# Where a block's score products stand: a RetNet and ELU-MLP kernel whose TensorE queue is full

## The chip, the cores and the metric

The kernel runs on one core of a Trainium2 chip. The metric is the time of one launch on the device, in microseconds (us); a version's time is the median over its runs. Everything is computed in 32-bit floating point.

## The reference

Two steps follow one another. The first is the recurrent form of retention, for 4 sequences of 768 tokens with 8 heads of 64:

```
for t in range(S):
    state = gamma * state + k[t] (outer product) v[t]      # per sequence and head, 64 x 64
    y[t]  = scale * q[t] @ state
```

with `gamma = 1 - 2 ** (-5 - h)` for head `h` and `scale = 1 / sqrt(64)`. The heads of a token are then put side by side, which gives a matrix `x` of 3072 tokens by 512. The second step is a two-layer perceptron with an ELU between its layers:

```
h = x @ w_in                                  # 512 -> 2048
g = where(h > 0, h, exp(min(h, 0)) - 1)
out = g @ w_out                               # 2048 -> 512
```

## The kernel before

**Blocks.** The 3072 tokens are cut into six blocks of 512 (`tb` 0 to 5; the text counts them from the first block, so the third block is `tb` 2). Each block is four chunks of 128 tokens, and a chunk is loaded as one 1024 KB transfer that holds q, k and v.

**Retention of a block** is done in pieces of 64 tokens and comes in five steps, which the function `retention_step(tb, step)` lists:

- step 0, scores: `scores(tb, pp)` for the two pairs of chunks, `pp` 0 and 1. Each makes 32 products of 64x64 on TensorE (L312) into two PSUM tiles `sc`, and two VectorE multiplications by the causal mask (L323) write the masked scores over the chunk's transposed k.
- step 1, states: 64x64 products k by v (L352) into PSUM tiles `kv`, and a chain of VectorE additions (L364) that sums the states of the pieces one after another.
- steps 2, 3 and 4, outputs: `outputs_step` multiplies scores by v (L408) and states by q (L423) into PSUM tiles `y`; small VectorE copies (`seen`, L392) stand in the first two steps, and in the last one four VectorE multiplications (L398) write the block's `x`.

The powers of gamma are put on v beforehand: `scale_v(m)` multiplies the v of chunk `m` by a table (L286), on VectorE for the third block and on GpSimd for later ones. The states of a block need its scaled v; the scores don't.

**The two GEMMs of a block** use Strassen's seven products, numbered 1 to 7, in one level or in two. In the second block the first GEMM is one level: `first(n)` for four slices `n` of w_in, each seven products of eight 128x256 matmul records (L758) in the order 1, 2, 6, 7, 5, 3, 4. The last two products of a slice are issued after the first two of the next slice. After each product ScalarE copies PSUM away (L704), VectorE adds (`h<-pd,m` and `h<-pb,m`, L709), ScalarE makes the exponential (L491, L492) and VectorE finishes the ELU (L495).

The second GEMM, `second_twice(tb, ...)`, has two levels: seven outer products in the order of `ORDER2`, 1, 2, 6, 7, 5, 3, 4, and in each of them seven inner ones of eight 128x128 records (L973). In what follows an outer product is called j1, j2, j6 and so on, and its inner ones k1, k2, k6, k7, k5, k3, k4; the last two again come after the first two of the next outer product. VectorE makes the sums of the inputs (`ts`, L847) and adds the results up (`res`, L985); between some outer products it also renews an input in place (L787). Each inner product takes a 256 KB piece of w_out from a ring of eleven buffers (`wq`), which SyncE fills.

**The order of the work** on each engine is the order in which the program is written: there is no scheduler. The third block's retention therefore stands where the code of the second block calls `retention_step(2, ...)`: at five visits in the second block's second GEMM, listed in `VISITS`. Later blocks have steps 0 and 1 inside their first GEMM (L931) and three visits in the second.

The PSUM tiles `sc`, `kv` and `y` rotate through a pool of four, `ps_r`. The GEMMs use four others: two named `pa`, one `pb` and one `pd`. A product that starts in `pd` has to wait until VectorE has read what was in it.

Of the kernel before, what the change touches and what calls it, by code (L numbers as in the profile page):

```python
# [18 lines left out]
def kernel(  # L19
# [45 lines left out]
    CPB = TB // C  # L65
# [33 lines left out]
    def load(m, cuts=(0, 2048), behind=None):  # L99

        if m >= NCHUNK:
            return
        t = ldpool.tile([P, 2048], FP32, name="chunk", tag="chunk")
        raw[m] = (
            t[:, 0:1024].rearrange("p (a h c) -> p a h c", a=2, c=C),
            t[:, 1024:2048].rearrange("p (a h d) -> p a h d", a=2, d=D),
        )
        hold(t, behind)
        for lo, hi in itertools.pairwise(cuts):
            nc.sync.dma_start(t[:, lo:hi], qkv[m, :, lo:hi])  # L110
# [169 lines left out]
    def scale_v(m, by_vector=False):  # L280
        if m >= NCHUNK:
            return
        i = chunks[m][1]
        v = raw[m][1][:, 0]
        eng = nc.vector if by_vector or m < 2 else nc.gpsimd
        eng.tensor_tensor(  # L286
            out=v, in0=v, in1=vf[:, i].unsqueeze(2).to_broadcast([C, H, D]), op=ALU.mult
        )
# [18 lines left out]
    def score_products(sc, tb, pp, x):  # L307
        qk = raw[tb * CPB + 2 * pp + x][0]
        for p in range(HP):
            for sub in range(2):  # L310
                for a in range(2):
                    nc.tensor.matmul(  # L312
                        sc[a][rows(sub), x, p, :], lhsT=qk[rows(a), 1, p, rows(sub)],
                        rhs=qk[rows(a), 0, p, rows(sub)], start=True, stop=True, skip_group_check=True,
                    )

    def scores(tb, pp):

        sc = [ps_r.tile([P, 2, HP, D], FP32, name="sc", tag="r") for _ in range(2)]
        for x in range(2):  # L320
            score_products(sc, tb, pp, x)
        for a in range(2):
            nc.vector.tensor_tensor(  # L323
                out=raw[tb * CPB + 2 * pp + a][0][:, 1].rearrange("p h c -> p (h c)").rearrange("p (n t) -> p n t", t=D),
                in0=sc[a].rearrange("p x h t -> p (x h) t"),
                in1=cmask.unsqueeze(1).to_broadcast([P, 2 * HP, D]), op=ALU.mult,
            )
# [38 lines left out]
    def states(tb, pp):  # L366

        kvs = [ps_r.tile([P, 2, HP, D], FP32, name="kv", tag="r") for _ in range(2)]
        for x in range(2):
            state_products(kvs, tb, pp, x, range(2))  # L370
        for x in range(2):
            for sub in range(2):
                state_sum(kvs, tb, pp, x, sub)
# [80 lines left out]
    def outputs_step(tb, step):  # L454

        if step == 0:
            held["y"] = [outputs(tb, pp) for pp in range(2)]
        if step < 2:
            next(held["y"][step])
            next(held["y"][step])  # L460
        else:
            for g in held["y"]:
                next(g, None)
# [18 lines left out]
    def flush():  # L482
        while later:
            later.pop(0)()
# [170 lines left out]
    def send_small():  # L655
        while to_send:
            nc.sync.dma_start(*to_send.pop(0))
# [41 lines left out]
    def bank(x):  # L699
        return ps_f.tile([P, 2, TH], FP32, name="p" + x, tag=x, bufs=2 if x == "a" else 1)  # L700
# [491 lines left out]
    def run(steps):  # L1192
        for _ in steps:
            pass
# [8 lines left out]
    def some(steps, count):  # L1203
        for _ in itertools.islice(steps, count):
            pass
# [78 lines left out]
    def retention_step(tb, step):  # L1284
        if tb >= NTB:
            return
        if step == 0:
            scores(tb, 0)
            scores(tb, 1)
        elif step == 1:  # L1290
            states(tb, 0)
            states(tb, 1)
        elif step < 5:
            outputs_step(tb, step - 2)
# [9 lines left out]
    for n in range(NQ):  # L1304
        if n < 3:
            load(2 * CPB + n)
        if n == 2:
            load(2 * CPB + 3)
        cur = first(n)
        for at in range(3):  # L1310
            next(cur)

        if n in (1, 2):
            some(smalls[n + 1], 1)
        elif n == 3:
            scale_v(2 * CPB, True)
        for _ in tail:
            pass
        for at, s in enumerate(cur):
            next(sides[n], None)  # L1320
            next(sides[n], None)
            if at == 1 and n in (0, 2):
                some(smalls[2 if n == 0 else 3], 2)
            elif at == 1 and n == 3:
                for m in range(1, CPB):
                    scale_v(2 * CPB + m, True)
            if s == "gap":
                break
        for _ in sides[n]:
            pass  # L1330
        tail = cur
        if n in (1, 2):
            run(smalls[n + 1])
        send_small()

    early.close()
    ring = ctx.enter_context(tc.tile_pool(name="ring", bufs=RING))
# [10 lines left out]
    for _ in tail:  # L1348
        pass
    flush()  # L1350
    step, VISITS = 0, [(0, "end"), (2, "middle"), (3, "first"), (4, "end"), (5, "end")]
    for s in sec:
        if s == "first":
            step += 1
        at = (step, s if s in ("first", "middle") else "end")
        if at in VISITS:
            retention_step(2, VISITS.index(at))
        if s == ORDER2[-1]:
            break
    tail = sec  # L1360
# [2 lines left out]
    for tb in range(2, NTB):  # L1363
        more = tb + 1 < NTB
        qa, qd, u2, end = {}, {}, {}, None

        def rest(n, j):
            if j == 1:
                qa[n] = ps_r.tile([P, 2, TH], FP32, name="qa", tag="r") if n == 0 else bank("a")
            if j == 7:  # L1370
                qd[n] = ps_r.tile([P, 2, TH], FP32, name="qd", tag="r") if n == 3 else bank("bd"[n % 2])
            first_rest(n, j, qa[n] if j in (1, 6, 5) else qd[n])

        def bring(n):
            if more:
                load((tb + 1) * CPB + n)
                scale_v((tb + 1) * CPB + n)

        def pop(count=1):
            for _ in range(count):  # L1380
                if later:
                    later.pop(0)()

        bring(0)
        rest(0, 1)
        for _ in tail:
            pass
        tail, parts = iter(()), combine_x_parts()
        for at, j in enumerate(TWICE):
            cur = first_twice(tb, j)  # L1390

            next(cur)
            next(tail, None)
            next(parts, None)
            next(cur)
            for _ in tail:
                pass
            next(parts, None)
            if at == 1:

                first_end(0, "C11", qa[0])()
                bring(1)
            next(cur)
            tail = cur
        next(tail)
        bring(2)

        sec = second_twice(tb, combine_x_twice if more else lambda: None)
        for n in range(NQ):

            rest(n, 6)
            u2[n] = kept(qa[n])
            if n == 0:
                for _ in tail:
                    pass
            if end:
                end()
            pop()
            rest(n, 7)
            m7 = kept(qd[n])  # L1420
            pop(2)
            if n == 2 and more:
                retention_step(tb + 1, 1)
            if n == 3:
                next(sec)
            rest(n, 5)
            end = first_end(n, "C12", qa[n])
            other = first_end(n, "C22", qa[n], m7)
            if n < 3:
                end()  # L1430
                other()
                rest(n + 1, 1)
                first_end(n + 1, "C11", qa[n + 1])()
                rest(n, 4)
                end = first_end(n, "C21", qd[n], u2[n])
                pop()
                if n == 0:
                    bring(3)
                elif n == 1 and more:
                    retention_step(tb + 1, 0)  # L1440
        for _ in range(2):
            next(sec)
        end()
        other()
        rest(3, 4)
        end = first_end(3, "C21", qd[3], u2[3])
        next(sec)
        end()
        flush()
        step = 0  # L1450
        for s in sec:

            if s == "first":
                step += 1
            elif s != "middle" and step in (1, 4, 5):
                retention_step(tb + 1, {1: 2, 4: 3, 5: 4}[step])
            if s == ORDER2[-1]:
                break
        tail = sec
# [51 lines left out]
```

## Time and profile before

| | us |
|---|---|
| median of 3 runs (lowest, highest) | 632.94 (632.79, 635.29) |
| the profiled execution | 633.48 |
| its span, first to last instruction | 631.6 |
| TensorE busy in the span | 623.8 |
| VectorE busy | 482.1 |
| ScalarE busy | 255.3 |
| GpSimd busy | 22.1 |

A time in the timeline is counted from the start of the span. A row of the timeline has the start, the duration, the engine, the line, the operation, the tiles written and read, the shape and the number of records that it merges; in brackets stands the idle time of the engine before it, and what ended it. Matmuls overlap, and their modelled ends lie a little past the start of the next one, so TensorE's own pace is read from the distance between starts. DVE is VectorE, ACT ScalarE, POOL GpSimd, PE TensorE, PEld its weight loads, and SP the queue of SyncE that issues the DMAs. Most products of a 32-bit matmul leave two records, so a product of four matmuls shows as eight.

### The profile page before, as it was taken

Reading aid. Unit: us, or ns where it says so; the run is one execution under the profiler, and the core shown is the slowest. Engines: PE = TensorE matmul, PEld = TensorE weight load, DVE = VectorE, ACT = ScalarE, POOL = GpSimd, SP = SyncE. Lnnn points to the kernel's source line nnn. Section 1 sums busy time; section 2 is a strip of 40 time slices with the busy share of each in tenths; the row PEclk is TensorE's granted clock in tenths of the full one; section 3 lists DMA queues with packets and bytes.
Section 4 is the critical chain, followed back from the end, with each engine's and each line's share of the span. In section 5 each row is a group of like instructions: output and inputs, shape, how many; then the busy total and the mean of one; then the engine's idle time right before and its main releaser. Section 6 shows DMA issues by size and latency. Waiting matters only on the chain.

```text
span 631.6 us, 16140 instructions
## 1 busy us (share of the span) xinstructions
PE 623.8 (99%) x6678; PEld 560.5 (89%) x6678; DVE 482.1 (76%) x882; ACT 255.3 (40%) x476; POOL 22.1 (4%) x30
## 2 busy tenths in 40 slices
PE   8999999999999999999999999999999999999997
PEld 6864578888899999888999989999989999988997
DVE  6688789989799665799585589777489877558975
ACT  6798646025541114553112646112465211366311
POOL 1021000000000000200000100000110000000000
PEclk9999999999999999999999999999999999999999
DMA  8698669699288788306888702889810698700794
GB/s 329 260 416 295 186 202 268 196 272 319 113 266 257 234 258 315 141 2 199 257 258 296 278 2 71 268 280 289 317 64 16 220 310 252 207 17 4 239 309 151
DMA packets 75897, 136.32 MB, mean 216 GB/s; under 512 B 6320, under 2 KB 31792, under 8 KB 70832
## 3 DMA queue, kind: packets, MB, share of 16 engines
q1 hardware_dynamic: 75824, 135.29, 64.9%
q8 instruction: 53, 0.87, 0.5%
q14 instruction: 20, 0.16, 0.1%
HBM read 114.03 MB, written 21.23 MB: 214 GB/s over the span
## 4 chain that ended last, share of the span: by engine, by line
PE 98%; DVE 0%; issue 0%; ACT 0%
PE pa L973 20%; PE pa L931 10%; PE pd L973 10%; PE pb L973 5%; PE pa L885 5%; PE pb L931 4%; PE pa L758 4%; PE pa L535 3%; PE qa L931 3%; PE x L625 3%; PE pd L885 2%; PE qd L931 2%; PE pd L931 2%; PE pd L758 2%; PE pa L625 2%; PE kv L352 2%
## 5 line engine op out<-in xcount | busy, mean ns | idle before, releaser
L981 ACT COPY ms<-pa 128x128 f32<-128x128 f32 x104 | 27.6, 265 | 148.2 <-PE pa L973 148.2
L973 PE MATMUL pa<-ts,wq 128*128 128x128 f32 x560 | 74.2, 275 | 0.0
L973 PE MATMUL pd<-ts,wq 128*128 128x128 f32 x552 | 73.5, 276 | 0.0
L973 PEld LDWEIGHTS pa<-ts,wq 128*128 128x128 f32 x560 | 68.5, 192 | 0.4
L973 PEld LDWEIGHTS pd<-ts,wq 128*128 128x128 f32 x552 | 67.1, 192 | 0.6 <-DVE res L985 0.2
L973 PE MATMUL pa<-gC,wq 128*128 128x128 f32 x480 | 64.6, 278 | 0.0
L492 ACT ACTIVATE r<-r 128x512 f32<-128x512 f32 x96 | 60.5, 631 | 3.1
L973 PEld LDWEIGHTS pa<-gC,wq 128*128 128x128 f32 x480 | 59.0, 192 | 1.3
L491 ACT ACTIVATE r<-gC 128x512 f32<-128x512 f32 x64 | 39.9, 624 | 31.9 <-DVE gC L939 31.9
L985 DVE TENSOR_TENSOR res<-pd,ms 128x128 f32<-128x128 f32 x68 | 19.5, 287 | 39.6 <-PE pd L973 38.4
L495 DVE SCALAR_TENSOR_TENSOR gC<-r,gC 128x512 f32<-128x512 f32 x64 | 42.6, 697 | 0.7 <-ACT r L492 0.7
L847 DVE TENSOR_TENSOR ts<-gC,ts 128x512 f32<-128x512 f32 x60 | 41.3, 688 | 1.0
L847 DVE TENSOR_TENSOR ts<-gC 128x512 f32<-128x512 f32 x60 | 41.0, 683 | 0.0
L286 POOL TENSOR_TENSOR chunk<-chunk,vf 128x512 f32<-128x512 f32 x16 | 19.4, 1212 | 429.6 <-DMA chunk<-in_qkv_dram 429.6
L973 PE MATMUL pb<-gC,wq 128*128 128x128 f32 x240 | 31.7, 275 | 0.0
L1006 ACT COPY res<-pa 128x128 f32<-128x128 f32 x34 | 9.0, 265 | 55.1 <-PE pa L973 55.1
L973 PEld LDWEIGHTS pb<-gC,wq 128*128 128x128 f32 x240 | 29.2, 192 | 0.0
L704 ACT COPY m<-pa 128x512 f32<-128x512 f32 x24 | 14.0, 582 | 33.0 <-PE pa L758 18.7
L939 DVE TENSOR_TENSOR gC<-qa,gC 128x512 f32<-128x512 f32 x8 | 5.5, 692 | 25.0 <-PE qa L931 18.3
L931 PE MATMUL pa<-xt,w_s 128*128 128x256 f32 x96 | 23.0, 382 | 0.0
L931 PE MATMUL pa<-xt,w_b 128*128 128x256 f32 x96 | 23.0, 382 | 0.0
L931 PE MATMUL pa<-xb,w_a 128*128 128x256 f32 x96 | 22.7, 379 | 0.0
(262 smaller groups left out, 1247.4 us busy)
## 6 DMA issues: line engine op xcount, KB each, us to landing
wq<-scratch_dram SPq DMA_DIRECT2D x277, 256.0 KB, 4.4
chunk<-in_qkv_dram SPq DMA_DIRECT2D x22, 1024.0 KB, 8.7
wraw<-in_w_dram SPq DMA_DIRECT2D x15, 1024.0 KB, 6.0
out_dram<-res SPq DMA_DIRECT2D x14, 256.0 KB, 4.1
scratch_dram<-gT SPq DMA_DIRECT2D x12, 256.0 KB, 4.3
scratch_dram<-m SPq DMA_DIRECT2D x12, 192.0 KB, 6.1
scratch_dram<-so SPq DMA_DIRECT2D x4, 512.0 KB, 4.7
scratch_dram<-wi SPq DMA_DIRECT2D x2, 1024.0 KB, 6.5
```

What stands on the lines that cost most here:

```text
L286: eng.tensor_tensor(out=v, in0=v, in1=vf[:, i].unsqueeze(2).to_broadcast([C, H, D]), op=ALU.mult)
L491: nc.scalar.activation(e, h, AF.Relu, scale=-1.0)
L492: nc.scalar.activation(e, e, AF.Exp, scale=-1.0)
L495: nc.vector.scalar_tensor_tensor(g, e, -1.0, h, ALU.add, ALU.max)
L625: nc.tensor.matmul(X[j][:, d, :], lhsT=w[j][:, d * P : d * P + P], rhs=x[j], start=(n == 0 and d == 0), stop=at_end, skip_group_check=True,)
L758: nc.tensor.matmul(ps[:, fi, :], lhsT=w[:, fi, j2, :], rhs=x[:, j2, :], start=(begin and fi == 0 and j2 == 0), stop=(j2 == 1), skip_group_ ...
L847: sub = lambda o, x, y: nc.vector.tensor_tensor(out=o, in0=x, in1=y, op=ALU.subtract)
L885: nc.tensor.matmul(ps[:, f, :], lhsT=lhs[f], rhs=xs[j][k], start=(begin and f == 0), stop=True, skip_group_check=True,)
L931: nc.tensor.matmul(ps[:, fi, :], lhsT=w[:, fi, j2, :], rhs=x[:, j2, :], start=(j in (1, 7) and fi == 0 and j2 == 0), stop=(j2 == 1), skip_ ...
L973: nc.tensor.matmul(ps, lhsT=w[:, f, :], rhs=ts[j][k][:, f, :], start=(begin and f == 0), stop=(f == 3), skip_group_check=True,)
L981: nc.scalar.copy(m, ps)
L985: nc.vector.tensor_tensor(out=o, in0=x, in1=y, op=ALU.add)
```

## The change

Three places of the program's last part are edited. In the second block's first GEMM the third block's scores are now issued in two halves: `scores(2, 0)` after slice 2's product 5, and `scores(2, 1)` in slice 3 between products 7 and 5. The place of the second half was that of the scaling of the chunks 9 to 11 (three multiplications, L286), which now stands after slice 3's product 5. In the second block's second GEMM four visits are left, for the steps 1 to 4. In the third block's second GEMM the first of the three output visits (for the fourth block) stands one outer product later; the blocks after it keep theirs.

```diff
@@ second block, first GEMM: for n in range(NQ) @@
             if at == 1 and n in (0, 2):
                 some(smalls[2 if n == 0 else 3], 2)
             elif at == 1 and n == 3:
-                for m in range(1, CPB):
-                    scale_v(2 * CPB + m, True)
+                scores(2, 1)
             if s == "gap":
                 break
...
         send_small()
+        if n == 2:
+            scores(2, 0)
+        elif n == 3:
+            for m in range(1, CPB):
+                scale_v(2 * CPB + m, True)
@@ second block, second GEMM @@
-    step, VISITS = 0, [(0, "end"), (2, "middle"), (3, "first"), (4, "end"), (5, "end")]
+    step, VISITS = 0, [(0, "end"), (2, "middle"), (3, "end"), (5, "end")]
     for s in sec:
         if s == "first":
             step += 1
         at = (step, s if s in ("first", "middle") else "end")
         if at in VISITS:
-            retention_step(2, VISITS.index(at))
+            retention_step(2, 1 + VISITS.index(at))
@@ later blocks, second GEMM @@
-        step = 0
+        step, visits = 0, (2, 4, 5) if tb == 2 else (1, 4, 5)
         for s in sec:
             if s == "first":
                 step += 1
-            elif s != "middle" and step in (1, 4, 5):
-                retention_step(tb + 1, {1: 2, 4: 3, 5: 4}[step])
+            elif s != "middle" and step in visits:
+                retention_step(tb + 1, 2 + visits.index(step))
```

The first visit of the second block's second GEMM thus holds the states where it held the scores, the second the first outputs where it held the states. The old third visit, near the start of outer product 7's inner ones, is gone; the second outputs stand three inner products after it, and the old fourth visit is gone too. The number of multiplications, additions and transfers is the same before and after.

## The prediction

> **What bounds the kernel now.** First the page: busy times and the chain that ended last.
>
> ```profile
> PE 623.8 (99%) x6678; PEld 560.5 (89%) x6678; DVE 482.1 (76%) x882; ACT 255.3 (40%) x476; POOL 22.1 (4%) x30
> ...
> PE 98%; DVE 0%; issue 0%; ACT 0%
> ```
>
> TensorE sets the time, and nothing that the edit moves leaves its queue. So the change is worth what it alters in TensorE's pauses. I read these from distances between starts, in the timeline. An undisturbed inner product (128x128) starts 0.893 us after the one before (188.72 to 198.55 us holds eleven); a 128x256 product of the first GEMM takes 1.727.
>
> VectorE and TensorE where the first GEMM hands over to the second:
>
> ```profile
> 175.21 1.89 DVE L286 TENSOR_TENSOR chunk<-chunk,vf 128x512 f32<-128x512 f32 x3
> 178.35 0.69 DVE L709 TENSOR_TENSOR h<-pd,m 128x512 f32<-128x512 f32 x1 [1.25 <-ACT m L704]
> 178.96 0.68 DVE L495 SCALAR_TENSOR_TENSOR gC<-r,h 128x512 f32<-128x512 f32 x1
> 179.56 0.69 DVE L847 TENSOR_TENSOR ts<-gC 128x512 f32<-128x512 f32 x1
> ...
> 182.09 0.28 DVE L985 TENSOR_TENSOR res<-pb,ms 128x128 f32<-128x128 f32 x1
> 182.29 0.68 DVE L495 SCALAR_TENSOR_TENSOR gC<-r,h 128x512 f32<-128x512 f32 x1
> 182.97 0.69 DVE L709 TENSOR_TENSOR h<-pd,m 128x512 f32<-128x512 f32 x1
> ```
>
> ```profile
> 182.77 1.05 PE L973 MATMUL pa<-ts,wq 128*128 128x128 f32 x8
> 183.72 1.16 PE L973 MATMUL pd<-ts,wq 128*128 128x128 f32 x8
> 184.72 1.06 PE L973 MATMUL pa<-ts,wq 128*128 128x128 f32 x8
> 185.70 2.10 PE L312 MATMUL sc<-chunk 64*64 64x64 f32 x128
> 187.73 1.16 PE L973 MATMUL pa<-gC,wq 128*128 128x128 f32 x8
> 188.72 1.06 PE L973 MATMUL pb<-gC,wq 128*128 128x128 f32 x8
> ```
>
> The three scalings (L286) lie in a hole: after them VectorE still idles 1.25 us. From 179.56 on it has no idle time until 197 us. The product at 183.72 (k7 of j1) writes `pd`, whose last content (slice 3's product 4) VectorE reads at 182.97; it starts 0.95 us after its forerunner, 0.06 late, and the next is late by 0.10 more, as after every pause. This is where delay of VectorE becomes delay of TensorE.
>
> The third block's first output visit holds a pause of another kind:
>
> ```profile
> 296.69 1.16 PE L408 MATMUL y<-chunk 64*64 64x64 f32 x64
> 297.68 0.52 PE L423 MATMUL y<-chunk 64*64 64x64 f32 x18
> 299.46 0.34 PE L423 MATMUL y<-chunk 64*64 64x64 f32 x6 [1.25 <-issue]
> ```
>
> No semaphore ends it. The records' starts are 297.98 and 299.46: 1.47 us. In the trace's DMA packets a 16 KB instruction packet (queue 8) starts at 297.22 and lasts 0.89; work resumes 2.24 us after its start.
>
> [...]
>
> **The change, part by part.**
>
> *Scores leave.* Products at 184.72 and 188.72 are 4.00 us apart with the visit between; less two periods it cost 2.21 us.
>
> *Two half visits arrive.* A half has 64 records fewer. In the first block 64 such records run from 20.12 to 21.10, 0.98 us; so a half costs 2.21 - 0.98 = 1.23, two 2.46. Net +0.25: one more pair of switches. The four masks: the first two come behind VectorE's work at 167.47 and end near 169.3, before slice 3's product 2 is done (169.17 + 1.23 = 170.4). The last two start when the second half is computed, near 178.4, and end near 179.6, before the C22 sum (178.35 + 2.46 = 180.81). They cost nothing on this path while these holes of 2 us last. No DMA is moved: SyncE's order is the same, and DMA is idle from 160 to 165 us, so the chunks issued by 149 have landed.
>
> *Scaling moves behind that sum.* It fell into a hole; now the C22 sum and its ELU stand first, and the three scalings hold up `ts`. `ts` starts at 178.96 + 0.60 + 2.46 + 3 x 0.60 = 183.83. Four sums (179.56 to 182.09: 2.53), `res` (0.20), an ELU (0.60): the read of `pd` starts at 187.16, and k7 0.75 after it (182.97 to 183.72), at 187.91. TensorE could start it at 182.77 + 2.46 + 0.89 = 186.12. A wait of 1.79, of which 0.06 was there: **+1.73**. Queued behind k7 is all of TensorE. k6 needs the second `ts` sum, ready near 185.2, when it is due; a wait there is swallowed by k7's.
>
> *States in the first visit.* TensorE pays for states what scores cost (198.55 to 202.54, less two periods: 2.20). VectorE has seven chained sums (201.39 to 204.62: 3.23) for four masks (188.96 to 191.36: 2.40), 0.83 more. Next is `res<-pd` of j1's k4 (before: 191.60), which frees `pd` for j2's k7 (192.29). Both now lie 4.19 later (187.91 - 183.72); VectorE's read moves to 191.36 + 0.20 + 4.19 + 0.83 = 196.58, and k7 follows such a read by 0.34 (294.37 to 294.71): 196.92 against 196.48. 0.44 and the restart of 0.10: **+0.54**. After that the renewals of C11 (L787) end some 0.4 us ahead of k2 of j6, and `res` at 197.86 had 0.63 idle: no third wait.
>
> *Outputs move up.* Three visits at unchanged price (1.75, 1.75, 1.29 from starts), behind states that are long summed; nothing.
>
> *Third block.* The fourth block's first outputs move past seven inner products. Counting records, block edges lie every 256 from the pause's record, 6593. The edge before, 6337, was crossed at 291.41. Now seven products (6.25 us) stand in between, and the edge falls 47 records into the visit, 12 us after the one before instead of 6.6. The packet started 5.8 us after that edge; 8.1 us suffice. The pause goes: **-1.47**. VectorE loses the visit's cover at 296.7, but its renewals end at 297.06, before the k2 that would then start at 297.5.
>
> Sum: 0.25 + 1.73 + 0.54 - 1.47 = **+1.05** on the profiled execution's 633.48 (span 631.6), which lies 0.54 above the median; I add it to the median: **634.0**.
>
> **Bounds.** VectorE's waits: nothing if TensorE's real dependence were looser (no evidence), at most 0.6 more for each further 512-wide operation in front. Fetch: before, packets in the two second GEMMs started 1.9 to 5.8 us after an edge (1.94, 4.88, 1.92, 2.29, 1.95, 4.77, 5.52, 5.81, 4.1), and 2.24 more are needed. In the second block the moved first outputs now contain edge 4289, 6.5 us after edge 4033; a start later than 4.3 makes a pause, up to 5.8 + 2.24 - 6.5 = 1.5. I take nothing, but it is close to even.
>
> **Rivals.** (1) *A new fetch pause at edge 4289*, typically 0.5 to 1.5: 634.5 to 635.5. For it: four of nine starts are late enough. Against: edges crossed in dense 64x64 stretches were followed quickly. (2) *The old pause isn't regained*, because timed runs don't have it (the profiled one is 0.54 slower than the median) or it turns up elsewhere: 632.94 + 2.52 = 635.5. (3) *Slower*: instruction packets come late as often as before, so that the old pause is not regained and edge 4289 pauses too: from 0.65 us of pause there the 0.5% line, 636.1, is passed; with 1.5 it is 637.0. (4) *The waits on `pd` don't come*, since VectorE catches up: 632.94 + 0.25 - 1.47 = 631.7. Against: its order is fixed and no idle time is left to remove.
>
> **How the numbers follow.** Forecast 0.40; (1) 0.23; (2) 0.17; (3) 0.12; (4) 0.08. About 0.5% (3.2 us) is what a measurement of this kernel can tell from no change. Forecast, (1), (2) and (4) lie inside it; (3) and a little of (2) beyond: slower 0.14, same 0.84, faster 0.02. Range 631.9 to 636.5: it leaves out half of (3) and the edge of (4).
>
> **What would show it.** Timeline after: k7 of j1 waiting for `h` L709 with 1.6 us of visible idle near 187.9, and a short wait of j2's k7 near 196.9; `ts` starting 183.8; no "issue" pause in the fourth block's first outputs; the first masks at 168.1. A TensorE without the first wait, or a pause inside an `sc` or `y` visit, makes the prediction wrong.

## The result, and the profile after

The changed kernel takes 635.85 us in the median of 22 runs (634.59 to 637.06), the kernel before 632.9 in 22 runs (632.26 to 636.28). The ratio is 1.0037 with a 95% interval of 1.0027 to 1.0047: 2.3 us slower (1.7 to 3.0). It agrees with the means, 635.79 and 633.45; the medians lie 2.95 apart, since some runs of the kernel before lie well above its median. So the change costs some 2.3 to 3 us, where 1.05 was forecast. That is inside the stated range and inside the half per cent that was called "same", above the forecast of 634.0, and close to rivals (1) and (2).

First the page of the profile after: busy times, and the chain that ended last.

```profile
PE 625.4 (99%) x6678; PEld 560.6 (88%) x6678; DVE 483.0 (76%) x882; ACT 255.8 (40%) x476; POOL 21.5 (3%) x30
...
PE 91%; DVE 3%; ACT 2%; issue 1%; DMA 1%; SPq 0%; DVEq 0%
```

The span is 634.5 us against 631.6. TensorE has the same 6678 matmul records and is still the chain, but 3% of it now runs through VectorE and 1% through "issue". Who it waited for is said by the list of waits, TensorE's own (total, times, longest):

```profile
...
PE pd L973 <- DVE h L709: 1.4, 1, 1.4
PE y L423 <- issue: 0.6, 1, 0.6
...
PE pd L973 <- DVE res L985: 0.3, 1, 0.3
```

These are the two waits of the prediction and one pause that it had put among the rivals. The timeline of VectorE at the hand-over between the two GEMMs, after:

```profile
182.06 0.69 DVE L709 TENSOR_TENSOR h<-pd,m 128x512 f32<-128x512 f32 x1 [1.18 <-ACT m L704]
182.67 0.68 DVE L495 SCALAR_TENSOR_TENSOR gC<-r,h 128x512 f32<-128x512 f32 x1
183.27 1.89 DVE L286 TENSOR_TENSOR chunk<-chunk,vf 128x512 f32<-128x512 f32 x3
185.07 0.69 DVE L847 TENSOR_TENSOR ts<-gC 128x512 f32<-128x512 f32 x1
...
188.41 0.68 DVE L709 TENSOR_TENSOR h<-pd,m 128x512 f32<-128x512 f32 x1
```

The three scalings (L286) now lie between the C22 sum at 182.06 and the first `ts` sum, which before followed the ELU directly. So the read of `pd` (188.41) comes late, and with it k7 of j1. TensorE, same kernel:

```profile
186.59 1.13 PE L973 MATMUL pa<-ts,wq 128*128 128x128 f32 x8
189.14 1.16 PE L973 MATMUL pd<-ts,wq 128*128 128x128 f32 x8 [1.43 <-DVE h L709]
190.14 1.06 PE L973 MATMUL pa<-ts,wq 128*128 128x128 f32 x8
191.12 2.08 PE L352 MATMUL kv<-chunk 64*64 64x64 f32 x112
...
196.81 1.06 PE L973 MATMUL pa<-ts,wq 128*128 128x128 f32 x8
198.13 1.16 PE L973 MATMUL pd<-ts,wq 128*128 128x128 f32 x8 [0.27 <-DVE res L985]
```

The starts 186.59 and 189.14 are 2.55 us apart, where 0.95 stood before. The second pair, 1.32 apart instead of 0.89, is j2's k7 behind the states' sums. VectorE shows these sums (L364) in front of the `res` that frees `pd`:

```profile
194.38 0.41 DVE L364 TENSOR_TENSOR chunk<-kv,carry 128x256 f32<-128x256 f32 x1
194.90 2.79 DVE L364 TENSOR_TENSOR chunk<-kv,chunk 128x256 f32<-128x256 f32 x6
...
197.80 0.28 DVE L985 TENSOR_TENSOR res<-pd,ms 128x128 f32<-128x128 f32 x1
```

The visits of outputs on TensorE: the third block's first outputs in the second block, and the fourth block's in the third.

```profile
206.65 0.23 PE L423 MATMUL y<-chunk 64*64 64x64 f32 x2
207.51 0.46 PE L423 MATMUL y<-chunk 64*64 64x64 f32 x16 [0.64 <-issue]
...
307.54 1.16 PE L408 MATMUL y<-chunk 64*64 64x64 f32 x64
308.53 0.63 PE L423 MATMUL y<-chunk 64*64 64x64 f32 x24
```

The fourth block's outputs, which paused for 1.47 us at 297.98 in the profile before, run through. The third block's, moved up, pause for 0.85 at 206.65.

One difference between the two profiles has nothing to do with the change. The last product that stands ahead of every changed instruction on TensorE, slice 2's product 5, starts 1.13 us later in the profile after (164.85 against 163.72), through pauses in the first 52 us. The first block's pauses differ between profiles of one kernel too: the second block's first product starts at 132.64, 132.66 and 133.25 us in three profiles of the kernel before. This difference is left out of the sums below.

### The profile page after: what moved, and what is told of

Same layout as the page of the kernel before. It is cut to its first block, busy times and chain, and to the rows that moved or that the text cites. A ratio compares the mean times of both kernels' runs of the same rounds, so it can differ in the third digit from the quotient of the medians.

```text
span 634.5 us, 16140 instructions
## 1 busy us (share of the span) xinstructions
PE 625.4 (99%) x6678; PEld 560.6 (88%) x6678; DVE 483.0 (76%) x882; ACT 255.8 (40%) x476; POOL 21.5 (3%) x30
## 4 chain that ended last, share of the span: by engine, by line
PE 91%; DVE 3%; ACT 2%; issue 1%; DMA 1%; SPq 0%; DVEq 0%
PE pa L973 19%; PE pa L931 10%; PE pd L973 10%; PE pb L973 5%; PE pa L885 5%; PE pb L931 4%; PE pa L758 3%; PE qa L931 3%; PE x L625 3%; PE pa L535 2%; PE pd L885 2%; PE qd L931 2%; PE pa L625 2%; PE pd L931 2%; PE y L408 2%; PE y L423 2%
## 5 line engine op out<-in xcount | busy, mean ns | idle before, releaser
L495 DVE SCALAR_TENSOR_TENSOR gC<-r,gC 128x512 f32<-128x512 f32 x64 | 44.3, 723 | 0.7 <-ACT r L492 0.7
L286 POOL TENSOR_TENSOR chunk<-chunk,vf 128x512 f32<-128x512 f32 x16 | 18.8, 1172 | 434.6 <-DMA chunk<-in_qkv_dram 201.5
```

What stands on the lines that cost most here:

```text
L286: eng.tensor_tensor(out=v, in0=v, in1=vf[:, i].unsqueeze(2).to_broadcast([C, H, D]), op=ALU.mult)
L495: nc.vector.scalar_tensor_tensor(g, e, -1.0, h, ALU.add, ALU.max)
```

## Experiments

Two things were to be told apart: whether the two waits have the causes given (the scalings in front of `ts`; seven state sums in the place of four masks), and what the "issue" pauses are and how often timed runs have them. The cost of a visit is taken throughout as in the prediction: the distance from the start of the product before it to the start of the second one after it, less two undisturbed periods.

**The third block's part alone.** The kernel before with this edit:

```diff
-        step = 0
+        step, visits = 0, (2, 4, 5) if tb == 2 else (1, 4, 5)
...
-            elif s != "middle" and step in (1, 4, 5):
-                retention_step(tb + 1, {1: 2, 4: 3, 5: 4}[step])
+            elif s != "middle" and step in visits:
+                retention_step(tb + 1, 2 + visits.index(step))
```

> The kernel before with one edit: the fourth block's first outputs stand seven inner products later in the third block's second GEMM; the second block is untouched. Theory 'pause in every run': the 1.47 us pause that the profiled execution of before had inside that visit goes, in timed runs too: ratio to before 0.9977. Theory 'pause in few runs': timed runs of before rarely have it, so the median doesn't move: 1.000 within 0.0005. Either way the profile shows no pause in the moved visit and no wait on pd beyond the old 0.06.

Measured: 632.64 us, ratio 0.9994 (0.9986 to 1.0002). The profile has no pause in the moved visit, which costs 1.75. The time lies between the two theories: the interval, -0.9 to +0.1 us, excludes a gain of 1.47 in every run, and doesn't settle a small gain. The old pause is not in all runs.

**The second block's part alone.** The changed kernel with the third block's visits put back:

```diff
-        step, visits = 0, (2, 4, 5) if tb == 2 else (1, 4, 5)
+        step, visits = 0, (1, 4, 5)
```

> The changed kernel with the third block's visits put back, so that only the second block differs from before. Both theories have the two VectorE waits here (1.71 and 0.53) and one more pair of switches (0.25): +2.49, with a fetch pause in the moved first outputs up to +3.35. 'Pause in every run': 1.47 us slower than the changed kernel, ratio to before 1.0060. 'Pause in few runs': as slow as the changed kernel, 1.0037 to 1.0042. The profile tells whether the old pause at the fourth block's first outputs is there again.

Measured: 636.42 us, ratio 1.0056 (1.0042 to 1.0071), 3.5 us slower than before; the sum with a pause in the moved outputs had been up to 3.35. In six runs that lies nearest to 'pause in every run' (1.0060), and the interval only just reaches 'pause in few runs' (1.0042). The third block's part alone had excluded a pause in every run, so the two together point to some of the runs. In its profile the third block's first outputs pause for 1.13 us, at the same record as in the changed kernel. The fourth block's first outputs stand where before had them and don't pause this time (TensorE's timeline):

```profile
301.81 1.16 PE L408 MATMUL y<-chunk 64*64 64x64 f32 x64
302.80 0.63 PE L423 MATMUL y<-chunk 64*64 64x64 f32 x24
```

**The kernel before, twice more.** No edit; two more profiles.

> The kernel before once more, a look. 'Pause in every run': the fourth block's first outputs cost 3.2 us instead of 1.75, as in the first profile. 'Pause in few runs': they cost 1.75, and the span is 1.5 us shorter or filled with other pauses of that kind elsewhere.

> As the look before it: 3.2 us for that visit if the pause is in every run, 1.75 if it is not.

The same visit in the first and in the second of them:

```profile
296.71 1.16 PE L408 MATMUL y<-chunk 64*64 64x64 f32 x64
297.71 0.52 PE L423 MATMUL y<-chunk 64*64 64x64 f32 x18
299.75 0.34 PE L423 MATMUL y<-chunk 64*64 64x64 f32 x6 [1.53 <-issue]
```

```profile
297.31 1.16 PE L408 MATMUL y<-chunk 64*64 64x64 f32 x64
298.30 0.63 PE L423 MATMUL y<-chunk 64*64 64x64 f32 x24
```

The first pauses for 1.75 us between starts; up to there its records run within 0.1 us of the first profile's of before, afterwards 0.3 behind them, and it took 633.68. The second doesn't pause and took 632.52. With the first profile and that of the second block's part alone, the pause is there in two of four executions that have this visit at this place. If timed runs have it as often, half of 1.47 is 0.7 us on average, an estimate from four executions; the interval of the third block's part alone holds it.

The trace's DMA packets tell what sets these executions apart. Between the edge before (record 6337, 256 ahead of 6593) and this one exactly one instruction packet (queue 8) starts in each of the four. In the two executions with the pause it starts at 297.22 and 296.89 us, and work resumes 2.24 and 2.86 after it. In the two without, the second further profile of before and the second block's part alone, it starts at 293.37 and 298.35 us, 5.2 and 4.7 before the edge is crossed.

**Scaling ahead of the masks.** The changed kernel with the scaling of the chunks 9 to 11 put back:

```diff
             elif at == 1 and n == 3:
+                for m in range(1, CPB):
+                    scale_v(2 * CPB + m, True)
                 scores(2, 1)
...
-        elif n == 3:
-            for m in range(1, CPB):
-                scale_v(2 * CPB + m, True)
```

> The changed kernel with the scaling of chunks 9 to 11 put back ahead of the second half of the scores, in the 1.88 us that VectorE idles there. Theory 'scaling in front of the input sums': k7 of j1 starts on time again, the wait of 1.59 and k6's 0.18 go, and the run is 1.7 us faster than the changed kernel: ratio to before 1.0010. The second wait, 0.43, stays, since the states still stand in the first visit. Rival 'masks are too many for VectorE': the hand-over stays late by more than 1 us, ratio 1.003.

Measured: 633.75 us, ratio 1.0011 (1.0004 to 1.0018), 2.1 us below the changed kernel's median (1.6 by the ratios; 1.7 was expected). VectorE first, then TensorE:

```profile
178.20 1.89 DVE L286 TENSOR_TENSOR chunk<-chunk,vf 128x512 f32<-128x512 f32 x3
180.10 1.29 DVE L323 TENSOR_TENSOR chunk<-sc,cmask 128x512 f32<-128x512 f32 x2
182.63 0.69 DVE L709 TENSOR_TENSOR h<-pd,m 128x512 f32<-128x512 f32 x1 [1.24 <-ACT m L704]
183.24 0.68 DVE L495 SCALAR_TENSOR_TENSOR gC<-r,h 128x512 f32<-128x512 f32 x1
183.84 0.68 DVE L847 TENSOR_TENSOR ts<-gC 128x512 f32<-128x512 f32 x1
```

```profile
187.05 1.05 PE L973 MATMUL pa<-ts,wq 128*128 128x128 f32 x8
188.00 1.16 PE L973 MATMUL pd<-ts,wq 128*128 128x128 f32 x8
...
197.00 1.16 PE L973 MATMUL pd<-ts,wq 128*128 128x128 f32 x8 [0.27 <-DVE res L985]
```

Scalings and masks together still leave 1.24 us of the hole unused, and `ts` follows the ELU again. k7 of j1 starts 0.95 us after k6, as in before: the first wait is gone. The second is unchanged, 0.44 late. The masks were never too many for VectorE; only the place of the scalings cost. The pause in the moved outputs was there too, at the same record, but with 0.31 instead of 0.85.

**The old places for the other visits.** The changed kernel with the first visit of the second block's second GEMM empty:

```diff
-    step, VISITS = 0, [(0, "end"), (2, "middle"), (3, "end"), (5, "end")]
+    step, VISITS = 0, [(2, "middle"), (3, "first"), (4, "end"), (5, "end")]
```

> The changed kernel with the first visit of the second block's second GEMM left empty and the states and the three outputs at the places that they had in before. Theory 'sum of the parts': the second wait (0.43 and 0.10) goes, and so does the fetch pause inside the moved first outputs (0.86 in the profiled execution); the first wait stays: 0.5 to 1.4 us faster than the changed kernel, ratio to before 1.0015 to 1.0029. Rival 'where the visits stand makes no difference': 1.0037.

Measured: 634.57 us, ratio 1.0031 (1.0019 to 1.0043), 1.3 us below the changed kernel in the medians; by the ratios 0.4, less than the 0.5 to 1.4 expected, with an interval that holds most of the theory's 1.0015 to 1.0029 and the rival's 1.0037 too, so the time alone decides little. The profile does:

```profile
186.45 1.13 PE L973 MATMUL pa<-ts,wq 128*128 128x128 f32 x8
189.01 1.16 PE L973 MATMUL pd<-ts,wq 128*128 128x128 f32 x8 [1.43 <-DVE h L709]
...
194.47 1.06 PE L973 MATMUL pa<-ts,wq 128*128 128x128 f32 x8
195.36 1.06 PE L973 MATMUL pd<-ts,wq 128*128 128x128 f32 x8
```

The first wait is the same within 0.01 us (2.56 between the two starts). The second is gone: j2's k7 follows k6 at 0.89. And the third block's first outputs cost 1.75, without a pause. States and outputs went back together here; the profile is what tells the two gains apart.

**Moving the edges.** The changed kernel with fewer and longer warm-up matmuls:

```diff
-    for n in range(25):
+    for n in range(15):
         nc.tensor.matmul(
-            (warm, other)[n % 2][rows(n // 2 % 2), 0:D], lhsT=blank[rows(n % 2), 0:D], rhs=blank[rows(n % 2), 0:D],
+            (warm, other)[n % 2][rows(n // 2 % 2), 0:107], lhsT=blank[rows(n % 2), 0:D], rhs=blank[rows(n % 2), 0:107],
...
```

> The changed kernel with 15 warm-up matmuls of 107 columns for 25 of 64 (as many columns), so that TensorE's instruction stream is 40 records shorter before the change's places. Theory 'instruction block edge': the edge of record 4290, which falls into the third block's first outputs, now falls just behind them into 128x128 products; their visit costs 1.75 again, no pause of 0.3 to 1.1 stands in it, and the run is 0.7 us faster than the changed kernel, ratio to before 1.0025. Rival 'a pause of the moved visit itself' (its data or PSUM tiles are late): the visit keeps a pause of 0.3 to 1.1, at the same matmul as before, ratio 1.0037.

Measured: 639.08 us, ratio 1.0091 (1.007 to 1.0111). The visit in question did what the theory of the edge says: it costs 1.75, with nothing inside. The time went the other way, by 3.2 us against the changed kernel's median. Part of what happened in the profiled execution (638.91 us) shows in the first block. TensorE's timeline there, and the windows of the same stretch (busy time and records of PE, PEld, DVE, ACT and POOL, granted clock, DMA share, GB/s):

```profile
24.03 0.62 PE L408 MATMUL y<-chunk 64*64 64x64 f32 x25
26.52 1.03 PE L408 MATMUL y<-chunk 64*64 64x64 f32 x36 [1.88 <-issue]
```

```profile
24.00:27.00 3.00, 1.12 (x51) 1.01 (x54) 1.09 (x3) 2.97 (x5) 0.00 (x0) 0.97 0.50 205
27.00:30.00 3.00, 2.70 (x90) 2.39 (x83) 0.84 (x3) 2.42 (x3) 0.00 (x0) 0.50 0.03 5
30.00:33.00 3.00, 3.00 (x14) 2.66 (x15) 2.31 (x4) 0.00 (x0) 0.00 (x0) 0.96 0.02 5
```

A pause of 2.09 us between starts stands at record 961 (22 x 256 ahead of 6593), and after it come 3.4 us at half the TensorE clock, an estimate from the clocks 0.97, 0.50 and 0.96 of the three windows; before had a clock of 1.00 in all three. A second pause of the kind, 0.77 us, stands at record 2242 (8 x 256 ahead of 4290). In the stream of records all later work has moved 40 places towards the start, but the pauses still stand where the count of records puts the edges. The distance to the packet is of the same size too: work resumes 2.52 and 2.33 us after the start of the one packet in between.

Why the clock fell isn't shown. Against the profile before, TensorE is 2.0 us back after the first pause and 3.3 at 30.4 us, at the end of the slow stretch; against that of the changed kernel, which has pauses of its own, 3.4 are left at the first score visit in the second block (170.1 instead of 166.7). But that doesn't explain the median. One such stretch lowers the mean clock of the execution to 0.997; the other five, 638.60 to 641.07 us, have 0.999 or 1.0 and are as slow without it. What slows them isn't shown, and the edit also makes the warm-up matmuls wider, so it isn't a pure shift.

**All scores in one early visit.** The changed kernel with both halves after slice 2's product 5, the scaling at its old place, and the visits of "old places":

```diff
             elif at == 1 and n == 3:
-                scores(2, 1)
+                for m in range(1, CPB):
+                    scale_v(2 * CPB + m, True)
...
         if n == 2:
             scores(2, 0)
-        elif n == 3:
-            for m in range(1, CPB):
-                scale_v(2 * CPB + m, True)
+            scores(2, 1)
...
-    step, VISITS = 0, [(0, "end"), (2, "middle"), (3, "end"), (5, "end")]
+    step, VISITS = 0, [(2, "middle"), (3, "first"), (4, "end"), (5, "end")]
```

> All of the third block's scores in one visit after slice 2's product 5, the scaling of chunks 9 to 11 at its old place, the other visits of the second block where before had them, and the third block's visits as in the changed kernel. Theory 'sum of the parts': no VectorE wait, since four masks (2.40) fit into the hole of about 1.0 that opens by 2.2 with the visit, no extra switches, no new edge inside a visit: the same time as the third block's part alone, ratio 0.999 to 1.000, thus 2.3 to 3 us faster than the changed kernel. Rival 'scores cost more early than late': slower than before by more than 0.5 us, ratio 1.001 or more.

Measured: 632.32 us in 22 runs (631.34 to 632.99), ratio 0.9983 (0.9973 to 0.9992): 1.1 us faster than before (0.7 in the medians) and 3.5 below the changed kernel's median. VectorE, then TensorE:

```profile
168.39 2.48 DVE L323 TENSOR_TENSOR chunk<-sc,cmask 128x512 f32<-128x512 f32 x4
172.06 0.69 DVE L709 TENSOR_TENSOR h<-pb,m 128x512 f32<-128x512 f32 x1 [1.19 <-PE pb L758]
```

```profile
185.31 1.05 PE L973 MATMUL pa<-ts,wq 128*128 128x128 f32 x8
186.26 1.16 PE L973 MATMUL pd<-ts,wq 128*128 128x128 f32 x8
```

All four masks fit, with 1.19 us left; the hand-over is as in before, and no visit pauses. The whole visit costs 2.23 us early, where it cost 2.21 late. The ratio lies a little below the 0.999 to 1.000 that was expected. The gain over before can be that of the third block's part (the interval, 0.5 to 1.7 us, holds the 0.7 of above, and overlaps with that of the part alone); whether something else adds to it isn't shown. So moving the scores early costs nothing here where it is done in one piece and in a hole.

## Why the prediction was right, and where its sizes were off

| term | predicted | in the profiles |
|---|---|---|
| scores leave, two halves arrive | +0.25 | +0.36 |
| scaling in front of `ts`: k6 and k7 of j1 | +1.73 | +1.71 |
| state sums in front of `res`: k7 of j2 | +0.54 | +0.53 |
| new pause in the third block's first outputs | 0 (rival 1) | +0.86 |
| old pause in the fourth block's first outputs | -1.47 | -1.47 in this pair; in two of four executions of that visit |

- *TensorE's visits.* A half visit costs 1.29, not 1.23: 0.06 more each. Scores, states and outputs otherwise kept their prices, wherever they stood.
- *The two waits.* k7 of j1 starts 2.55 us after k6 instead of 0.95, 1.60 more, and k6 itself comes 0.11 late, right behind the second `ts` sum. Their sum, 1.71, was right to 0.02. Less the shift of 1.13 that the profile after has from its start, `ts` began at 183.9 (predicted 183.8) and k7 at 188.0 (187.9). The experiments remove each wait by removing its cause while the other wait stays: the scalings for the first, the states' place (with that of the outputs) for the second.
- *No third wait.* There was none; nor was there one in the third block, where VectorE lost the cover of a visit.
- *The terms of the instruction packets failed in size.* The step "the pause goes: -1.47" took for certain what one profile showed. With two further profiles of before and one of the second block's part it is there in two of four executions, so it was worth an estimated 0.7. And the step "I take nothing, but it is close to even" for edge 4289 was wrong: the pause stands at record 4290 in all three profiles whose moved outputs contain that edge, with 0.31, 0.85 and 1.13 us. The prediction's own bound fits: by it, an estimate from one pause, a packet that starts later than 4.3 us after edge 4033 makes a pause. In the profile after edge 4033 is crossed at 200.14 and the packet starts at 205.01, 4.87 later; the sum of the bound then gives 0.6.

With the measured terms, 0.36 + 1.71 + 0.53 + 0.86 - 0.7 gives +2.8, inside the interval of 1.7 to 3.0. The same terms give the others: 0.36 + 2.24 + 1.13 = 3.7 for the second block alone (measured 3.5), 0.36 + 0.53 + 0.31 - 0.7 = 0.5 with the scaling first (0.7), 0.36 + 1.71 - 0.7 = 1.4 at the old places (2.0, interval 1.2 to 2.7). The pauses are from single profiles and four executions, so the agreement is that of an estimate. It was rival (1) together with half of rival (2), a milder form of rival (3), which had both in full; rival (4) didn't come about.

The range and "same" held because the range had been drawn wide enough for the rivals; the forecast itself missed by more than its size. By the prediction's last sentence "a pause inside an `sc` or `y` visit" makes it wrong, and one came, at 206.65. So its account of VectorE and its queue stands (waits of 1.73 and 0.54 us predicted, 1.71 and 0.53 measured). Of the instruction packets its bound for a late one held at edge 4289 in the profile after (a start 4.87 us after the edge before, a pause of 0.85), and the two sizes that it put into the sum, 0 and -1.47, don't stand.

That TensorE waits for late instruction packets in these pauses is the author's reading of the traces. The edges themselves are a count: the page of before has

```profile
q8 instruction: 53, 0.87, 0.5%
```

that is 53 packets of 16 KB each, and the trace has 13,612 records of TensorE (matmuls, weight loads and semaphores), 257 to a packet. The reading rests on four things: no semaphore ends the pauses; they stand at records a multiple of 256 apart, to within one (4290 and 6593, 961 and 2242), also where the work in front has become 40 records shorter; the pause in the third block's first outputs was gone in the one profile in which the edge lay behind them; and work resumes 2.24 to 2.86 us after the start of the one packet that comes in between, while the same edge is crossed without a pause where that packet started 4.7 us or more ahead. What decides when a packet starts in a given execution stays open; it wasn't tried to change the transfers that run beside it.

## What to carry to other kernels

On a full engine, an edit that moves work without adding any was priced here by the queues beside it (1.71 and 0.53 us of waits for VectorE) and by where an edge of 256 records falls (a pause of 0.85): list what each other engine now does in front of the one read that frees the next buffer, and check whether the hole it came from is still a hole. A piece of work that fits an idle stretch should be moved whole and together with what already lived there. And a pause seen in one profile is a sample: look at a second and third profile before its removal is booked as a gain.

## What was not expected of the hardware

A pause of 2.09 us at record 961, an edge in the count of 256, inside a dense 64x64 stretch, was followed by some 3.4 us at half the TensorE clock (0.50 from 27 to 30 us) in one profiled execution. And profiles of one program don't agree on such pauses: of three profiles of the kernel before, two cross the edge at record 6593 with pauses of 1.47 and 1.75 us and the third without one.
